# w2 in transfers of 8, 4 and 1 blocks, and the result on every eighth partition

## The chip, the core and the metric

The kernel runs on one core of a Trainium2 chip. A core has five engines that run their own instruction streams and meet at semaphores: TensorE (PE in the profile, its weight loads PEld), VectorE (DVE), ScalarE (ACT), GpSimd (POOL) and SyncE (SP, which here only issues transfers), beside 16 DMA engines that move data between the chip's memory (HBM) and the core's on-chip memory. The metric is device time in microseconds of one execution, the median of several.

## What is computed

One decode step of a transformer block for four sequences: attention over a cache of 4096 keys and values in 32 heads, then a dense layer with a mish activation. `_A` is the attention, `_B` the dense layer; the change touches only `_B` and the end of the kernel.

```python
B, Sq, D, F = 4, 1, 640, 1728;  H, Sk, Dh = 32, 4096, 128

def _A_ref(x, k_cache, v_cache, wq, wo):
    q = (x @ wq).reshape(B, Sq, H, Dh).transpose(0, 2, 1, 3)
    scores = einsum("bhqd,bhkd->bhqk", q, k_cache) * (Dh ** -0.5)
    o = einsum("bhqk,bhkd->bhqd", softmax(scores), v_cache)
    return o.transpose(0, 2, 1, 3).reshape(B, Sq, H * Dh) @ wo

def _B_ref(x, w1, b1, w2):
    h = einsum("bsd,df->bsf", x, w1) + b1
    sp = log1p(exp(-abs(h))) + where(h > 0, h, 0)
    return einsum("bsf,fd->bsd", h * tanh(sp), w2)

h  = x + _A_ref(layernorm(x), k_cache, v_cache, wq, wo)
h2 = h + _B_ref(layernorm(h), w1, b1, w2)          # the output, 4 x 640, bf16
```

## The kernel before

**Staging.** K and V are 268 MB of the 283 MB that the kernel reads. They pass through three large on-chip buffers (`slot`), 8 MB per transfer, in units of 8 heads of one sequence; 16 units in all. Per unit VectorE multiplies K with the query (L677), TensorE sums the products (L689), softmax follows (L726 to L774), and TensorE multiplies with V (L799). The steady part of this runs in hardware loops.

**The order of work** is written out by hand. The class `Program` records operations with what they read and write, works out the semaphore waits from that, and emits each engine's operations in the order in which they were added. So the order in the code is the order on each engine. All loads of weights and of K and V are issued from SP and go through one DMA queue, in the order of issue.

**The end of the kernel** reuses two of the slots. `wend` takes wo and w1, `wend2` takes w2 and, behind it, all small intermediate tiles (`scratch`). The weights are asked for by `load` (L907), which waits until the slot's readers are done and issues the transfer from SP (L916): wo in two parts, w1 in three, then the last 64 rows of w2 (L941, after a memset on GpSimd at L935 that clears the other partitions), then w2's 13 full blocks of 128 rows.

**How w2 lies.** F = 1728 rows are 13 blocks of 128 (`C2`) and 64 more. `W2P` says which blocks one transfer takes: 0 to 5, 6 to 9, 10 and 11, 12. Blocks go in pairs: a pair is 256 rows, and partition p holds rows 2p and 2p + 1 of it, so a row of the transfer is 2 x 640 bf16 values, 2,560 bytes in one piece. A block is thus every second row of 256. Block 12 and the rest are whole.

**What has to agree with it.** The activations of block c must lie on the partitions on which w2's rows of block c lie. `f_rows(c)` (L546) gives those rows as a slice; it is used where b1 is turned (L608, at the start of the kernel) and where w1 is applied: `h1_pass` (L1089) takes `w1_sb[:, dc, f_rows(c)]` as the stationary operand, 14 blocks for each of 5 chunks of D, 70 matmuls with 4 columns to stream (one for each sequence). The slices step by 2 elements (4 bytes) for blocks 0 to 11 and by 1 for the others. `d_rows` (L475) does the same for w1's own rows.

**From w1 to the output.** `hT` holds the residual sum h, transposed (L1059); its column means and variances come through TensorE (L1074). The w1 pass runs on TensorE around the variance, then the residual is put into the accumulator `y2` (L1164), then VectorE and ScalarE compute mish into `act_t` (L1123 to L1151, the last is one of the two instructions at L1134). A small matmul (L1192) and a ScalarE copy (L1196) move the last 64 activations to every second partition. Then `w2_products` (L1173): for each block four matmuls, one for each quarter of the 640 output columns, which go to partitions 32t to 32t + 3 of `y2`, for t = 0 to 3. The order is blocks 0 to 5, the rest, 6 to 9, 10 and 11, 12. Four copies, two on VectorE and two on ScalarE (`gather`, L1204), bring the quarters side by side onto four partitions, and SP stores them (L1213).

Of the kernel before, what the change touches and what calls it, by code (L numbers as in the profile page):

```python
# [8 lines left out]
BF16 = mybir.dt.bfloat16  # L9
ACT = mybir.ActivationFunctionType  # L10
ALU = mybir.AluOpType
# [223 lines left out]
def kernel(  # L235
# [13 lines left out]
    nc = tc.nc  # L249

    B, Sq, D = A_x.shape
    _, H, Sk, Dh = A_k_cache.shape
    F = B_w1.shape[1]
    N = B * Sq
    DC = D // 128
# [23 lines left out]
    C2 = F // 128  # L279
    FM = C2 * 128  # L280
    FREM = F - FM
    FC = C2 + 1
    W2P = (0, 6, 10, 12, C2)
    W1P = (0, 2, 4, DC)
    OT4 = 4
    DT = D // OT4
    OVER = 128 - FREM


# [14 lines left out]
    s_bank, tr_bank, qq_bank, o_bank, oT_bank = banks[0:4], *banks[4:8]  # L304
    S_BANK, TR, QQ, OB, OT = [("bank", i) for i in range(4)], *[("bank", i) for i in range(4, 8)]
# [5 lines left out]
    ident_f = const([128, 128], FP32, "ident_f")  # L311
# [48 lines left out]
    def load_kv(what, rows, u, i, parts=1):  # L360
        w = SLOT // parts
        for k in range(parts):
# [26 lines left out]
        w=cells(0, 0, o0),  # L389
# [5 lines left out]
        w=["b1"],  # L395
# [10 lines left out]
            out=ident[:, :],  # L406
            in_=ident[:, :],
# [6 lines left out]
        r=["ident"],  # L414
        w=["ident"],
# [4 lines left out]
        r=["ident"],  # L420
        w=["ident_f"],
# [12 lines left out]
    def bn_stats():  # L434
        for s in range(2):
# [7 lines left out]
        r=["stats"],  # L443
        w=["mv"],
# [4 lines left out]
            out=ln_std[:, :], in_=ln_mv[:, 1:2], func=ACT.Sqrt, bias=eps_t[0:N, :], scale=1.0  # L449
        ),  # L450
        r=["mv", "eps"],
        w=["std"],
# [4 lines left out]
        r=["std"],  # L457
        w=["rstd1"],
# [4 lines left out]
            out=ln1_bf,  # L463
# [6 lines left out]
        r=["x", "mv", "rstd1"],  # L470
        w=["ln1"],
# [12 lines left out]
    def turn_rows(src):  # L484
        for c in range(DC):
# [9 lines left out]
            out=q_sel[:, :, :],  # L495
            in_=ident[:, :].rearrange("p (t r) -> p t r", t=CT)[:, :, 0:N],
        ),
        r=["ident"],
        w=["q_sel"],
    )  # L500
    for src, dst, r, w in (
# [7 lines left out]
            r=[OT],  # L509
            w=[w],  # L510
# [3 lines left out]
    def identity_sums(dst, pattern, name, **kw):  # L514
# [13 lines left out]
            out=own[:, :], in0=own1[:, :], scalar1=-1.0, scalar2=1e30, op0=ALU.add, op1=ALU.mult  # L528
        ),
        r=["own1"],  # L530
        w=["own"],
# [7 lines left out]
        r=["dq_f"],  # L539
        w=["dq_m"],  # L540
# [3 lines left out]
    )  # L544

    def f_rows(c):  # L546
        if c < C2 - C2 % 2:
            f0 = c // 2 * 256 + c % 2
            return slice(f0, f0 + 255, 2)
        f0 = c * 128 if c < C2 else F - 128  # L550
        return slice(f0, f0 + 128)


    assert CT == NO
# [15 lines left out]
    for k in range(HC):  # L570
# [4 lines left out]
                out=q_rows[:, k * 512 : (k + 1) * 512], in_=s_bank[k][:, :]  # L575
            ),
            r=[S_BANK[k]],
            w=[("qrows", k)],
# [3 lines left out]
    def q_turned():  # L582
        for g in range(G):
# [14 lines left out]
            out=qT[:, 0 : NU * G].rearrange("p (o b g) -> p o b g", o=NO, b=N),  # L598
            in_=qT_ps[:, :, :, :].rearrange("p g o b -> p o b g"),
        ),  # L600
        r=[QQ],
        w=["qT"],
# [292 lines left out]
    i1, i2, i3 = slot_of(NU - 1), slot_of(NU - 2), slot_of(NU - 3)  # L895
    wend, wend2 = slot[i1], slot[i2]
# [4 lines left out]
    nw2 = FC * D  # L901
    w2_sb = wend2[:, 0 : C2 * D].rearrange("p (k n) -> p k n", k=C2)
    w2r_sb = wend2[:, C2 * D : nw2]
    C2E = C2 - C2 % 2
    w2_view = B_w2[0 : C2E * 128, :].rearrange("(m p k) n -> p m (k n)", p=128, k=2)

    def load(out_ap, in_ap, i, lo, hi, name, sem=None):  # L907


        ops = {}  # L910
        for cell in cells(i, lo, hi):
            for d in P.readers.get(cell, {}).values():
                ops[d.nth] = d
        P.add(
            "SP",
            lambda: nc.sync.dma_start(out=out_ap, in_=in_ap),  # L916
            w=[name],
            sem=sem or "_".join(map(str, name)),
            after=ops.values(),
        )  # L920
# [3 lines left out]
    for k0, k1 in zip(W1P, W1P[1:]):  # L924
# [11 lines left out]
        w=["w2r"],  # L936
# [5 lines left out]
        w=["w2r"],  # L942
        sem=f"slot{i2}",
    )
    for k0, k1 in zip(W2P, W2P[1:]):
        if k0 < C2E:
            assert k0 % 2 == k1 % 2 == 0
            to = wend2[:, k0 * D : k1 * D].rearrange("p (m n) -> p m n", n=2 * D)
            of = w2_view[:, k0 // 2 : k1 // 2]
        else:  # L950
            to, of = w2_sb[:, k0, :], B_w2[k0 * 128 : k1 * 128, :]
        load(to, of, i2, k0 * D, k1 * D, ("w2", k0))

    at = [nw2]

    def scratch(n, dt=FP32):
        a = at[0]
        w = n * (2 if dt == FP32 else 1)
        w += w % 2
        at[0] = a + w  # L960
        ap = wend2[:, a : a + w]
        return ap.bitcast(FP32)[:, 0:n] if dt == FP32 else ap[:, 0:n]

    def do(eng, emit, r=(), w=()):

        return P.add(eng, emit, r=r, w=w, after=[last_pv])
# [88 lines left out]
    def cols(n=DC, dt=FP32):  # L1055
        return scratch(n * N, dt).rearrange("p (c n) -> p c n", c=n)

    hT = cols()
    tt(hT, xT_res[:, :, :], yT[:, :, :], ALU.add, ["xT_res", S_BANK[0]], ["hT"])  # L1059

    def column_means(src, name):
        part = scratch(N)
        m_ps = oT_bank[:, 0:N]
        do(
            "DVE",
            lambda: nc.vector.tensor_reduce(
                out=part, in_=src.rearrange("p c n -> p n c"), axis=AX.X, op=ALU.add
            ),
            [name],
            [name + "_part"],  # L1070
        )
        do(
            "PE",
            lambda: nc.tensor.matmul(m_ps, lhsT=mean_f[:, :], rhs=part, start=True, stop=True),  # L1074
            [name + "_part", "mean_f"],
            [OT],
        )
        return m_ps

    m_ps = column_means(hT, "hT")  # L1080
    h2T, hc, sq = cols(dt=BF16), cols(), cols()
    for dst, w in ((h2T, "h2T"), (hc, "hc")):
# [17 lines left out]
    for dc in range(DC):  # L1100
        w1 = ("w1", max(k0 for k0 in W1P if k0 <= dc))
        do("PE", lambda dc=dc: h1_pass(dc), [w1, "h2T"], [QQ])
        if dc == 1:
# [4 lines left out]
                    out=std, in_=v_ps, func=ACT.Sqrt, bias=eps_t[:, :], scale=1.0  # L1108
# [10 lines left out]
            do("DVE", lambda: nc.vector.reciprocal(out=rstd, in_=std), ["std2"], ["rstd"])  # L1119

    h1n, h1s, ta, tb, tc_, td = (cols(FC) for _ in range(6))
    act_t = cols(FC, BF16)
    tt(  # L1123
        h1n, h1_ps, rstd.unsqueeze(1).to_broadcast([128, FC, N]), ALU.mult, [QQ, "rstd"], ["h1n"]
    )
# [5 lines left out]
    def stt(out_, a, scalar, b, op0, op1, r, w):  # L1131
        do(
            "DVE",
            lambda: nc.vector.scalar_tensor_tensor(  # L1134
                out=out_, in0=a, scalar=scalar, in1=b, op0=op0, op1=op1
            ),
            r,
            w,
        )
# [5 lines left out]
            out=tc_, in0=tb, scalar1=-0.5, scalar2=-1.0, op0=ALU.mult, op1=ALU.add  # L1145
# [2 lines left out]
        ["tc"],  # L1148
    )
    do("DVE", lambda: nc.vector.reciprocal(out=td, in_=tc_), ["tc"], ["td"])  # L1150
    stt(act_t, td, 1.0, h1s, ALU.add, ALU.mult, ["td", "h1s"], ["act"])  # L1151


    y2 = s_bank[1][:, 0:DT]

    def residual():
        for t in range(OT4):
            for c in range(DC):
                d0, step = d_rows(c).start, d_rows(c).step
                p0 = max(0, -(-(t * DT - d0) // step))  # L1160
                p1 = min(128, -(-((t + 1) * DT - d0) // step))
                if p0 < p1:
                    d = d_rows(c, p0, p1)
                    ins = nc.tensor.matmul(  # L1164
                        y2[32 * t : 32 * t + N, d.start - t * DT : d.stop - t * DT : step],
                        lhsT=hT[:, c, :],
                        rhs=ident_f[:, p0:p1],
                        start=(d.start == t * DT),
                        stop=False,
                    )  # L1170
        return ins

    def w2_products(blocks):  # L1173
        for c in blocks:
            w2, h = (w2_sb[:, c, :], act_t[:, c, :]) if c < C2 else (w2r_sb, act_r)
            for t in range(OT4):
                ins = nc.tensor.matmul(
                    y2[32 * t : 32 * t + N, :],
                    lhsT=h,
                    rhs=w2[:, t * DT : (t + 1) * DT],  # L1180
                    start=False,
                    stop=(c == C2 - 1),
                )
        return ins

    do("PE", residual, ["hT", "ident_f"], [S_BANK[1]])

    act_r = scratch(N, BF16)
    r_ps = oT_bank[:, 0:N]
    do(  # L1190
        "PE",
        lambda: nc.tensor.matmul(r_ps, lhsT=apart, rhs=act_t[:, C2, :], start=True, stop=True),  # L1192
# [3 lines left out]
    do("ACT", lambda: nc.scalar.copy(out=act_r, in_=r_ps), [OT], ["act_r"])  # L1196
    for k0, k1 in zip(W2P, W2P[1:]):
        do("PE", lambda b=range(k0, k1): w2_products(b), [("w2", k0), "act"], [S_BANK[1]])
        if k0 == 0:
            do("PE", lambda: w2_products([C2]), ["w2r", "act_r"], [S_BANK[1]])  # L1200
    out_bf = scratch(D, BF16)[0:N, :]

    def gather(t, copy):
        return lambda: copy(  # L1204
            out=out_bf[:, t * DT : (t + 1) * DT], in_=y2[32 * t : 32 * t + N, :]
        )

    for t in range(OT4):
        eng, copy = (("DVE", nc.vector.tensor_copy), ("ACT", nc.scalar.copy))[t % 2]
        do(eng, gather(t, copy), [S_BANK[1]], [("out_bf", t)])  # L1210
    P.add(
        "SP",
        lambda: nc.sync.dma_start(out=out.rearrange("b s d -> (b s) d"), in_=out_bf),  # L1213
        r=[("out_bf", t) for t in range(OT4)],
        sem="out",
    )

# [41 lines left out]
```

## Time and profile before

| | |
|---|---|
| median of 3 runs | 664.91 us (664.72 to 665.21) |
| the profiled execution | 664.55 us |
| its span, first to last instruction | 662.8 us |
| read from HBM in the span | 283.35 MB, 428 GB/s |
| PE / DVE / ACT / POOL busy, share of the span | 58% / 53% / 14% / 0% |
| TensorE's granted clock, mean | 0.804 |

The profile is of one execution. Its rows give start and duration in microseconds from the start of the span, engine, source line, operation, and the tiles written and read with their shapes (partitions x elements). "idle before" tells how long the engine stood before the instruction and what ended that. A granted clock of 0.50 means that TensorE had half of its full speed. The chain of waits is followed back from the last instruction: at each step to what released it. The columns of the windows are: the stretch and its length, busy time and number of instructions of PE, PEld, DVE, ACT and POOL, granted clock, share of the DMA engines, GB/s.

The weights of the end, as they are issued and land (from the list of DMA issues and SP's timeline):

| transfer | KB | issued at, us | us to landing |
|---|---|---|---|
| w2, last 64 rows | 80 | 625.42 | 28.7 |
| w2, blocks 0 to 5 | 960 | 626.01 | 30.5 |
| w2, blocks 6 to 9 | 640 | 626.64 | 31.5 |
| w2, blocks 10 and 11 | 320 | 637.54 | 21.5 |
| w2, block 12 | 160 | 646.3 | 13.1 |

### The profile page before, as it was taken

Reading aid. Unit: us, or ns where it says so; the run is one execution under the profiler, and the core shown is the slowest. Engines: PE = TensorE matmul, PEld = TensorE weight load, DVE = VectorE, ACT = ScalarE, POOL = GpSimd, SP = SyncE. Lnnn points to the kernel's source line nnn. Section 1 sums busy time; section 2 is a strip of 40 time slices with the busy share of each in tenths; the row PEclk is TensorE's granted clock in tenths of the full one; section 3 lists DMA queues with packets and bytes.
Section 4 is the critical chain, followed back from the end, with each engine's and each line's share of the span. In section 5 each row is a group of like instructions: output and inputs, shape, how many; then the busy total and the mean of one; then the engine's idle time right before and its main releaser. Section 6 shows DMA issues by size and latency. Waiting matters only on the chain.

```text
span 662.8 us, 6698 instructions
## 1 busy us (share of the span) xinstructions
PE 381.4 (58%) x2692; PEld 171.6 (26%) x2692; DVE 352.6 (53%) x315; ACT 90.3 (14%) x321; POOL 2.8 (0%) x14
## 2 busy tenths in 40 slices
PE   0364868375481837548183754818375481837675
PEld 0121323132230313223031322303132230313344
DVE  2085868184573818457381845738184572818502
ACT  0202020202002020200202020020202002020211
POOL 1000000000000000000000000000000000000000
PEclk9778889879695987969598796958879695887955
DMA  9999999999999999999999999999999999999997
GB/s 380 443 440 439 443 405 427 444 431 440 435 427 419 443 439 431 435 439 427 423 443 427 443 435 431 423 435 439 431 435 439 427 423 443 431 439 435 409 421 288
DMA packets 6685, 283.52 MB, mean 428 GB/s; under 512 B 713, under 2 KB 913, under 8 KB 2066
## 3 DMA queue, kind: packets, MB, share of 16 engines
q1 hardware_dynamic: 6664, 283.35, 99.2%
q8 instruction: 8, 0.13, 0.1%
q14 instruction: 3, 0.02, 0.0%
q10 hardware_dynamic: 10, 0.01, 0.0%
HBM read 283.35 MB, written 0.01 MB: 428 GB/s over the span
## 4 chain that ended last, share of the span: by engine, by line
DMA 44%; DVE 25%; PE 19%; another core or an unknown queue 6%; issue 2%; SPq 2%; ACT 1%; DVEq 0%; POOL 0%; ACTq 0%
DMA slot<-in_A_k_cache_dram 41%; DVE slot L677 21%; PE bank L689 13%; PE bank L799 5%; DMA slot<-in_B_w_dram 3%; DVE s_sb L664 3%; SPq L916 2%; ACT e L774 1%; PE bank L757 0%; DVE mx L744 0%; DVE rl L851 0%; PE bank L735 0%; DVE otn L858 0%; DVEq L228 0%
## 5 line engine op out<-in xcount | busy, mean ns | idle before, releaser
L689 PE MATMUL bank<-slot,ident 128*128 128x512 bf16 x1024 | 273.6, 422 | 242.3 <-DVE slot L677 242.3
L677 DVE TENSOR_TENSOR slot<-slot,qb 128x4096 bf16<-128x4096 bf16 x128 | 288.3, 2284 | 152.5 <-DMA slot<-in_A_k_cache_dram 148.1
L689 PEld LDWEIGHTS bank<-slot,ident 128*128 128x128 bf16 x1024 | 101.2, 107 | 399.9 <-DVE slot L677 274.7
L664 DVE TENSOR_REDUCE s_sb<-bank 128x64 f32<-128x512 f32 x64 | 44.0, 688 | 58.3 <-PE bank L689 58.3
L774 ACT ACTIVATE e<-s_sb,nb 128x256 bf16<-128x256 f32 x128 | 63.1, 494 | 44.2 <-DVE nb L766 44.2
L799 PE MATMUL bank<-slot,e 128*32 128x512 bf16 x1024 | 61.8, 395 | 4.4 <-DMA slot<-in_A_v_cache_dram 2.7
L644 ACT CAST qb<-bank 128x128 bf16<-128x128 f32 x17 | 4.5, 266 | 307.5 <-PE bank L635 307.5
L799 PEld LDWEIGHTS bank<-slot,e 128*32 128x32 bf16 x1024 | 26.6, 99 | 37.7 <-issue 9.6
L819 ACT COPY o_sb<-bank 128x512 f32<-128x512 f32 x16 | 9.4, 586 | 183.4 <-PE bank L799 183.4
L744 DVE TENSOR_REDUCE mx<-bank 1x8 f32<-1x128 f32 x16 | 4.5, 278 | 39.9 <-PE bank L735 39.9
L774 ACT ACTIVATION_READ_ACCUMULATOR e<-s_sb,nb 128x1 f32 x128 | 23.8, 186 | 0.0
L832 PE MATMUL bank<-sel,o_sb 128*128 128x8 f32 x136 | 18.5, 262 | 0.0
L832 PEld LDWEIGHTS bank<-sel,o_sb 128*128 128x128 f32 x136 | 17.4, 200 | 0.0
L851 DVE RECIPROCAL rl<-bank 128x8 f32<-128x8 f32 x17 | 3.4, 202 | 15.4 <-PE bank L832 15.4
L561 PE MATMUL bank<-slot,xT 128*32 128x512 bf16 x40 | 4.5, 631 | 10.7 <-DMA slot<-in_A_wq_dram 10.7
L757 PE MATMUL bank<-mx,nscale 1*128 1x8 f32 x32 | 6.1, 262 | 5.9 <-DVE mx L744 5.9
L618 DVE COPY b1T<-bank 128x14 f32<-128x14 f32 x1 | 0.2, 173 | 15.1 <-PE bank L608 15.1
L830 PEld LDWEIGHTS bank<-rs,ones_f 128*128 128x128 f32 x34 | 6.5, 197 | 3.8 <-ACT o_sb L819 1.6
L757 PEld LDWEIGHTS bank<-mx,nscale 1*128 1x128 f32 x32 | 4.7, 182 | 10.6 <-DVE mx L744 10.6
L726 DVE TENSOR_REDUCE pm<-s_sb 128x1 f32<-128x256 f32 x16 | 6.7, 420 | 0.5
L735 PE MATMUL bank<-ident_f,pm 128*1 128x128 f32 x32 | 6.1, 272 | 1.2 <-DVE pm L726 1.2
L766 DVE TENSOR_TENSOR nb<-bank,own 128x8 f32<-128x8 f32 x16 | 2.7, 167 | 7.6 <-PE bank L757 7.6
(85 smaller groups left out, 68.8 us busy)
## 6 DMA issues: line engine op xcount, KB each, us to landing
slot<-in_A_v_cache_dram SPq DMA_DIRECT2D x2, 4096.0 KB, 44.6
slot<-in_A_wq_dram SPq DMA_DIRECT2D x1, 5120.0 KB, 15.3
slot<-in_A_wo_dram SPq DMA_DIRECT2D x2, 2560.0 KB, 32.8
slot<-in_B_w_dram SPq DMA_DIRECT2D x2, 864.0 KB, 33.1
slot<-in_B_w_dram SPq DMA_DIRECT2D x1, 960.0 KB, 30.5
slot<-in_B_w_dram SPq DMA_DIRECT2D x1, 640.0 KB, 31.5
slot<-in_B_w_dram SPq DMA_DIRECT2D x1, 432.0 KB, 32.3
slot<-in_B_w_dram SPq DMA_DIRECT2D x1, 320.0 KB, 21.5
```

The lines of the kernel that those rows point to most:

```text
L664: lambda: nc.vector.tensor_reduce(out=s_sb[:, part * RP : (part + 1) * RP], in_=s_bank[part][:, :].rearrange("p (r w) -> p r w", w=W), axi ...
L677: return nc.vector.tensor_tensor(out=kt, in0=kt, in1=qbs[u % NS][:, k * DQ : (k + 1) * DQ] .unsqueeze(1) .to_broadcast([128, RP, DQ]), op= ...
L689: ins = nc.tensor.matmul(s_bank[part][:, :].rearrange("p (r w) -> p r w", w=W), lhsT=ident[:, :], rhs=kt[:, :, d : d + W], start=(d == 0), ...
L726: lambda: nc.vector.tensor_reduce(out=pm[:, :], in_=s_sb[:, :], axis=AX.X, op=ALU.max),
L735: lambda: nc.tensor.matmul(tr_bank[0:1, 0:128], lhsT=pm[:, :], rhs=ident_f[:, :], start=True, stop=True),
L757: lambda: nc.tensor.matmul(nb_ps, lhsT=nscale[:, :], rhs=mx[:, :], start=True, stop=True),
L774: ins = nc.scalar.activation(out=e2[:, :, h, :], in_=s_sb[:, :].rearrange("p (g r) -> p g r", r=RQ), func=ACT.Exp, bias=nb[:, h : h + 1], ...
L799: ins = nc.tensor.matmul(o_bank[t : t + G * RQ, :], lhsT=e2[:, g, :, :], rhs=vt[:, g * RQ : (g + 1) * RQ, :], start=(g < CT), stop=(g >= N ...
L819: lambda: nc.scalar.copy(out=o_sb[:, :], in_=o_bank[:, :]),
L830: nc.tensor.matmul(l_ps, lhsT=ones_f[:, :], rhs=rss[u % NS][:, :], start=True, stop=True)
L832: ins = nc.tensor.matmul(o_ps, lhsT=o_sb[:, r * Dh : (r + 1) * Dh], rhs=sel[:, r, :], start=(r == 0), stop=(r == RQ - 1),)
L916: lambda: nc.sync.dma_start(out=out_ap, in_=in_ap),
```

## The change

w2's full blocks go in three transfers, of 8, 4 and 1 blocks. In a transfer of n blocks, partition p holds n consecutive rows of w2, so its piece is n x 1,280 bytes. `f_rows` follows from the same table: it steps by 8, 4 and 1 elements.

The stationary operands of the residual and of the w2 products become 32 columns wide, zero but for every eighth column, which holds one of the four sequences. They come from two new tiles that GpSimd clears: `hW`, into which GpSimd copies `hT`, and `act_t`, which is now 32 wide itself and is written by VectorE with a step. So the products fill all 128 partitions of `y2`, and sequence b's quarter t lies on partition 32t + 8b. One copy on ScalarE takes all of `y2` out, and the store picks every eighth partition.

```diff
-    W2P = (0, 6, 10, 12, C2)
+    W2P = (0, 8, 12, C2)
...
+    OS = 32 // N
...
     def f_rows(c):
-        if c < C2 - C2 % 2:
-            f0 = c // 2 * 256 + c % 2
-            return slice(f0, f0 + 255, 2)
-        f0 = c * 128 if c < C2 else F - 128
-        return slice(f0, f0 + 128)
+        for k0, k1 in zip(W2P, W2P[1:]):
+            if k0 <= c < k1:
+                return slice(k0 * 128 + c - k0, k1 * 128 - (k1 - 1 - c), k1 - k0)
+        return slice(F - 128, F)
...
     for k0, k1 in zip(W2P, W2P[1:]):
-        if k0 < C2E:
-            assert k0 % 2 == k1 % 2 == 0
-            to = wend2[:, k0 * D : k1 * D].rearrange("p (m n) -> p m n", n=2 * D)
-            of = w2_view[:, k0 // 2 : k1 // 2]
-        else:
-            to, of = w2_sb[:, k0, :], B_w2[k0 * 128 : k1 * 128, :]
-        load(to, of, i2, k0 * D, k1 * D, ("w2", k0))
+        load(
+            wend2[:, k0 * D : k1 * D],
+            B_w2[k0 * 128 : k1 * 128, :].rearrange("(p k) n -> p (k n)", p=128),
+            i2, k0 * D, k1 * D, ("w2", k0),
+        )
...
+    hW = scratch(DC * 32).rearrange("p (c n) -> p c n", c=DC)
+    act_t = scratch(FC * 32, BF16).rearrange("p (c n) -> p c n", c=FC)
+    for t, name in ((hW, "hW"), (act_t, "act")):
+        do("POOL", lambda t=t: nc.gpsimd.memset(t, 0.0), w=[name])
     hT = cols()
     tt(hT, xT_res[:, :, :], yT[:, :, :], ALU.add, ["xT_res", S_BANK[0]], ["hT"])
...
+    do("POOL", lambda: nc.gpsimd.tensor_copy(out=hW[:, :, ::OS], in_=hT), ["hT", "hW"], ["hW"])
...
-    act_t = cols(FC, BF16)
...
-    stt(act_t, td, 1.0, h1s, ALU.add, ALU.mult, ["td", "h1s"], ["act"])
+    stt(act_t[:, :, ::OS], td, 1.0, h1s, ALU.add, ALU.mult, ["td", "h1s", "act"], ["act"])
...
-                        y2[32 * t : 32 * t + N, d.start - t * DT : d.stop - t * DT : step],
-                        lhsT=hT[:, c, :],
+                        y2[32 * t : 32 * t + 32, d.start - t * DT : d.stop - t * DT : step],
+                        lhsT=hW[:, c, :],
...
-                    y2[32 * t : 32 * t + N, :],
+                    y2[32 * t : 32 * t + 32, :],
...
-    act_r = scratch(N, BF16)
-    r_ps = oT_bank[:, 0:N]
+    act_r = scratch(32, BF16)
+    r_ps = oT_bank[:, 0:32]
...
-    out_bf = scratch(D, BF16)[0:N, :]
-
-    def gather(t, copy):
-        return lambda: copy(
-            out=out_bf[:, t * DT : (t + 1) * DT], in_=y2[32 * t : 32 * t + N, :]
-        )
-
-    for t in range(OT4):
-        eng, copy = (("DVE", nc.vector.tensor_copy), ("ACT", nc.scalar.copy))[t % 2]
-        do(eng, gather(t, copy), [S_BANK[1]], [("out_bf", t)])
+    out_bf = scratch(DT, BF16)
+
+    do("ACT", lambda: nc.scalar.copy(out=out_bf, in_=y2), [S_BANK[1]], ["out_bf"])
     P.add(
         "SP",
-        lambda: nc.sync.dma_start(out=out.rearrange("b s d -> (b s) d"), in_=out_bf),
-        r=[("out_bf", t) for t in range(OT4)],
+        lambda: nc.sync.dma_start(
+            out=out.rearrange("b s (t n) -> t (b s) n", t=OT4),
+            in_=out_bf[::OS, :],
+        ),
+        r=["out_bf"],
         sem="out",
     )
```

More of the change, by code (lines that the diff above doesn't have):

```diff
@@ L903 @@
     w2r_sb = wend2[:, C2 * D : nw2]
-    C2E = C2 - C2 % 2
-    w2_view = B_w2[0 : C2E * 128, :].rearrange("(m p k) n -> p m (k n)", p=128, k=2)
     def load(out_ap, in_ap, i, lo, hi, name, sem=None):
@@ L945 @@
     for k0, k1 in zip(W2P, W2P[1:]):
-        if k0 < C2E:
-            assert k0 % 2 == k1 % 2 == 0
-            to = wend2[:, k0 * D : k1 * D].rearrange("p (m n) -> p m n", n=2 * D)
-            of = w2_view[:, k0 // 2 : k1 // 2]
-        else:
-            to, of = w2_sb[:, k0, :], B_w2[k0 * 128 : k1 * 128, :]
-        load(to, of, i2, k0 * D, k1 * D, ("w2", k0))
+        load(
+            wend2[:, k0 * D : k1 * D],
+            B_w2[k0 * 128 : k1 * 128, :].rearrange("(p k) n -> p (k n)", p=128),
+            i2,
+            k0 * D,
+            k1 * D,
+            ("w2", k0),
+        )
     at = [nw2]
@@ L1184, in w2_products @@
         return ins
-    do("PE", residual, ["hT", "ident_f"], [S_BANK[1]])
-    act_r = scratch(N, BF16)
-    r_ps = oT_bank[:, 0:N]
+    do("PE", residual, ["hW", "ident_f"], [S_BANK[1]])
+    act_r = scratch(32, BF16)
+    r_ps = oT_bank[:, 0:32]
     do(
```

## The prediction

> **What bounds the kernel now.** I read the DMA row of the page first, then the chain of waits, then the timeline of the last ten microseconds.
>
> ```profile
> DMA  9999999999999999999999999999999999999997
> ```
>
> The 16 DMA engines are busy from the first slice to the last: 283.35 MB at 428 GB/s. Nothing in the change touches the loop over K and V or its bytes, so whatever it does happens in the last slice. The chain of waits ends there:
>
> ```profile
> 637.54 21.46 DMA slot<-in_B_w_dram
> 659.04 0.74 PE bank L1177 x12
> 659.81 0.31 DVE slot L1204
> 660.13 0.32 DVE slot L1204
> ```
>
> The columns are start, duration and what. The end is set by the last landings of w2, the last three rounds of w2 products, then two copies one behind the other on VectorE. After them comes the store. The timeline, on its way there:
>
> ```profile
> 652.29 0.89 PE L1091 MATMUL bank<-slot,slot 128*128 128x4 bf16 x28 [0.36 <-DVE slot L969]
> 653.46 1.26 PE L1091 MATMUL bank<-slot,slot 128*128 128x4 bf16 x42
> 654.65 1.01 PE L1164 MATMUL bank<-ident_f,slot 128*4 128x80 f32 x22
> 656.61 0.22 DVE L1134 SCALAR_TENSOR_TENSOR slot<-slot 128x56 bf16<-128x56 f32 x1
> 656.93 0.16 PE L1192 MATMUL bank<-slot 128*128 128x4 bf16 x1 [1.27 <-issue]
> 657.02 2.73 PE L1177 MATMUL bank<-slot 128*4 128x160 bf16 x56
> 658.23 0.36 PEld L1177 LDWEIGHTS bank<-slot 128*4 128x4 bf16 x16 [0.44 <-DMA slot<-in_B_w_dram]
> 659.04 0.10 PEld L1177 LDWEIGHTS bank<-slot 128*4 128x4 bf16 x8 [0.45 <-DMA slot<-in_B_w_dram]
> 659.45 0.09 PEld L1177 LDWEIGHTS bank<-slot 128*4 128x4 bf16 x4 [0.31 <-DMA slot<-in_B_w_dram]
> 660.48 0.34 SPq L1213 DMA_DIRECT2D out_dram<-slot  x1
> ```
>
> Two paths meet in the w2 products. One is the arithmetic: the w1 pass (L1091), the activation, ready at 656.61 + 0.22 = 656.83, and from 657.02 the products. The other is the landing of w2: TensorE waits for blocks 6 to 9 until 658.23, for 10 and 11 until 659.04, for block 12 until 659.45. The first six blocks are there at 656.5 (issued at 626.01, 30.5 to land), 0.3 us before the activation. So the arithmetic trails the data by little, and a delay of it is soon on the path.
>
> **The change, part by part.**
>
> *w2 in larger pieces.* 12 blocks now come in rows of 2,560 B. They will come in rows of 10,240 B (8 blocks) and 5,120 B (4). What row length is worth is read from the windows over stretches in which one kind of row was moving (wo in 20 KB, w1 in 6.9 KB, then w2); the last two columns are the share of the DMA engines and GB/s:
>
> ```profile
> 644.00:648.50 4.50, 2.30 (x84) 2.22 (x84) 0.30 (x1) 0.00 (x0) 0.00 (x0) 0.50 0.99 416
> 648.50:651.50 3.00, 2.45 (x81) 2.37 (x81) 0.36 (x2) 0.00 (x0) 0.00 (x0) 0.50 0.98 399
> 653.00:657.00 4.00, 2.73 (x74) 2.39 (x71) 1.75 (x7) 1.89 (x4) 0.00 (x0) 0.50 1.04 395
> ```
>
> GB/s over share gives 420 for 20 KB, 407 for 6.9 KB, 380 for w2. Eight blocks are 1.31 MB: 3.45 us at 380, 3.17 at 413 (10 KB, between the two rows). Four blocks: 0.66 MB, 1.72 against 1.66 at 395. That is 0.34 us less; bounds 0.2 (all at 395) and 0.5 (all at 420). The landings become: blocks 0 to 7 midway between 656.5 and 658.23, less 0.28, at 657.09; 8 to 11 at 659.04 - 0.34 = 658.70; block 12 at 659.11. SP issues one transfer fewer; it stands 10.46 us in an issue at 626.64, but the engines stay full meanwhile, so I count nothing.
>
> *The products.* 56 matmuls as before, in rounds of four that run side by side. Seven rounds go from 657.02 to about 658.12, one takes 0.33 (659.45 to 659.78): 0.13 us a round and 0.19 for the first to come through. Their weights grow from 4 to 32 columns. L799 already has 32-column weights: 32 matmuls of 512 in 3.61 us at clock 0.50, (3.61 - 0.19) / 8 = 0.43 a round, which is 0.13 for 160 columns. So 0; at most 56 x 14 ns = 0.8 us, by the mean load of 118 ns at L799 against 104 at L1177.
>
> *The result.* Two copies in turn on each of two engines, 659.81 to 660.46, become one ScalarE copy of 128x160. Between 266 ns (128x128, L644) and 586 (128x512, L819) that is 293 ns. PE's end to the store's issue shrinks from 0.70 to 0.34: 0.36 saved.
>
> *The store.* 16 pieces of 320 B in place of 4 of 1,280 B; its 5 KB stay. Issue 0.34 us, then 1.95 to the end of the span. I take it as equal, with bounds of -0.1 and +0.2 from the spread of issue times (0.33 at L366 to 0.56 at L385). The Trainium skill ("DMA: Bandwidth & Descriptors", Specifications) says that below 512 B the engine reads, modifies and writes; no run here shows its price, and the sum leaves it out.
>
> *GpSimd.* Two memsets after 625.9 (0.2 to 0.5 us each by L973 and L426; GpSimd then has nothing until 651) and one copy of hT at 651.07, some 0.26 us (L976). The residual that needs it starts at 654.65, so 3 us cover it. At worst the copy holds up VectorE's sum at 651.10 by 0.26. The SP queue's load of w2's last rows waits for the memset at L935, which stays ahead of the new ones.
>
> *The residual.* 22 matmuls in 1.01 us, weights 32 columns wide instead of 4. Loads of 128 four-byte columns take 227 ns at the same clock (L832: eight in 1.83); a quarter is 57, against some 30 now: +0.6 us at most. PE is idle from 655.66 to 656.90, which hides it, and that gap moves along with the w1 pass.
>
> *The columns of w1.* This is the part that the short description does not name. w1's columns must meet w2's rows, so f_rows now steps by 8 elements (16 B) for blocks 0 to 7, by 4 (8 B) for 8 to 11, and by 1 after; it was 2 and 1. The w1 pass loads these columns as weights, 5 x 14 = 70 loads of 128 columns with 4-column matmuls, so the load is the whole time: (1.26 - 0.17) / 41 = 27 ns each, with steps 2 and 1 alike. PE runs it without a gap from 652.29 to 654.65 ahead of the activation. One place in the trace has a wider step, L486 at the start: five loads with a step of 5 elements (10 B), then five with 2 and 1.
>
> ```profile
> 4.38 0.35 PE L486 MATMUL bank<-ident,slot 4*128 4x4 bf16 x5 [4.38 <-DVE slot L462]
> 5.09 0.27 PE L486 MATMUL bank<-ident,slot 4*128 4x4 bf16 x5 [0.36 <-DVE xT L508]
> ```
>
> With 178 and 162 ns for a single one, that is (0.35 - 0.18) / 4 = 43 ns a load against 27. A step of 10 B costs 16 ns more. Carried on in a line (2.7 ns per byte beyond 4), 16 B gives 59 and 8 B 38; in proportion to the step, 69 and 34. Then 40 loads x 32 to 42 + 20 x 7 to 11 = 1.5 to 1.8 us; I take 1.6. Bounds: 0 (the price has nothing to do with the step), and 114 ns a load, half of the 227 ns of a four-byte load, for all 60: 60 x 87 = 5.2 us. The Trainium skill speaks against the change here: "SBUF — State Buffer", Door 1, has lines of 16 B and wants at least two hits on each. A step of 16 B leaves one hit; if a load then takes twice 27 ns and a step of 8 B stays free, the delay is 1.1 us and the whole change comes to 0. L486 agrees in direction.
>
> The same step is in b1's turn (L608, 14 loads in 0.41 us at 21.5): +0.5 us, and the first multiplication waits for K until 35.42, so 0.
>
> **The sum.** Data path: blocks 8 to 11 at 658.70, five rounds 0.65 + 0.19 + 0.02, so products end at 659.56; copy and hand-over 0.34, store at 659.90, 0.58 earlier than 660.48. Arithmetic path with a w1 delay d: first product at 657.02 + d, 14 rounds 1.82 + 0.19, end 659.03 + d, store at 659.37 + d. It decides from d = 0.53. With d = 1.6 the store is issued at 660.97, 0.49 us later than now. Against the profiled execution's 664.55 that is 665.04; that execution lies 0.36 below the median of 664.91, so I forecast 665.4. What w2 and the copy gain (about 1.1 us on the arithmetic path) is given back by w1's loads.
>
> **The rivals.**
> 1. *The step is free or cheap*: at most L486's 16 ns for any wide step, d of 0 to 0.96. For it: steps 1 and 2 cost the same 27 ns. Against it: L486 itself. -0.58 to -0.15, 664.3 to 664.8.
> 2. *The wide step makes the load one column at a time* (slower). 114 ns a load for 40 of them, d = 40 x 87 = 3.5: +2.4 us, 667.3; for 60, +4.1, 669.0. It decides by more than 0.2% from d = 2.44, 88 ns a load. For it: the step grows far beyond any row of this trace. Against it: at 10 B the load is still well below 114.
> 3. *The store is longer by its small pieces*: at its own issue-to-end of 2.29 us, if pieces double the 1.95 that follows the issue, +1.95 on the sum, 667.4; half of that, 666.4. For it: nothing in the trace; against: 5 KB in all.
> 4. *w2's rows are cut up again and land as now*: the data path then ends only 0.36 earlier than today, and the sum, set by the arithmetic, stays at 665.4; the page's count of packets under 8 KB would stay at 2,066.
>
> **How the numbers follow.** 0.2% of the time is 1.33 us, about what a measurement of this kernel can tell from no change. Forecast (50 to 88 ns a load at the wide step, -0.1 to +1.3): 0.45, within 0.2%. Rival 1: 0.15, of it 0.04 faster by more. Rival 2: 0.32, slower. Rival 3: 0.06, of it 0.04 slower. Rival 4: 0.02, no change. Faster 0.04, same 0.60, slower 0.36. The range runs from rival 1's low end, 664.2, to 667.6, just past the first value of rival 2; the likeliest case's own range is 664.8 to 666.2.
>
> **What would show it.** L1091 (then by its new line) is the test: 70 loads over 2.1 us now, some 3.7 with the forecast, 5.6 with rival 2. The products should then run in one piece with no wait for w2 inside; waits for DMA there speak for rival 1. The copy should take 0.29, the store stay at 2.3 us to the end. Wrong altogether if the loop's first 620 us differ.

## The result and the profile after

The changed kernel takes 666.06 us (median of 22 runs, 665.6 to 668.05) against 664.90 us of the kernel before (22 runs): a ratio of 1.0017, with a 95% interval of 1.0010 to 1.0023. That is 1.16 us slower, within the 0.2% named in the prediction, and clear of its own interval.

The profiled execution is a long one, 667.25 us with a span of 665.4, so the two spans should not be subtracted. Of their 2.6 us, 1.57 lie before the landing of the second half of wo (TensorE takes it up at 650.13, before at 648.56). They arise in the loop over K and V: wo's first half is asked for at 612.73, before at 610.72. The change touches only one operation ahead of that, the turn of b1 at the start: it takes 0.82 us instead of 0.50, and the first multiplication, which waits for K, still starts at 35.36 (before at 35.42). The forecast's sign of being wrong altogether, a difference in the first 620 us, does not hold either: with the same b1 and the same loop, e2_w2_only asks for wo at 610.45 and e10_rows at 610.90 (both below). So the late start is this execution's own, and the runs leave open where it comes from; 1.2 us is also what this execution has over its median. From wo's landing on the two can be compared. Two rows of the kernel before that are needed for it (start, duration, engine, line, operation):

```profile
648.56 2.29 PE L1025 MATMUL bank<-slot,slot 128*128 128x4 bf16 x80 [2.26 <-DMA slot<-in_A_wo_dram]
...
654.76 0.22 DVE L969 TENSOR_TENSOR slot<-bank,slot 128x56 f32<-128x56 f32 x1 [0.64 <-PE bank L1091]
```

The timeline of the changed kernel:

```profile
650.13 2.29 PE L1024 MATMUL bank<-slot,slot 128*128 128x4 bf16 x80 [3.53 <-DMA slot<-in_A_wo_dram]
...
653.87 1.49 PE L1096 MATMUL bank<-slot,slot 128*128 128x4 bf16 x28 [0.36 <-DVE slot L968]
...
655.64 2.15 PE L1096 MATMUL bank<-slot,slot 128*128 128x4 bf16 x42
...
657.72 1.21 PE L1168 MATMUL bank<-ident_f,slot 128*32 128x80 f32 x22
657.82 0.22 DVE L968 TENSOR_TENSOR slot<-bank,slot 128x56 f32<-128x56 f32 x1 [1.53 <-PE bank L1096]
...
659.62 0.41 DVE L1138 SCALAR_TENSOR_TENSOR slot<-slot 128x56 bf16<-128x56 f32 x1
...
660.09 0.21 PE L1196 MATMUL bank<-slot 128*128 128x32 bf16 x1 [1.17 <-DVE slot L1138]
...
660.23 2.06 PE L1181 MATMUL bank<-slot 128*32 128x160 bf16 x56
...
662.34 0.29 ACT L1207 CAST slot<-bank 128x160 bf16<-128x160 f32 x1 [1.82 <-PE bank L1181]
662.66 0.68 SPq L1210 DMA_DIRECT2D out_dram<-slot  x1
```

The two parts of the w1 pass are 0.60 and 0.89 us longer than the 0.89 and 1.26 before. The write of the activation takes 0.41 where it took 0.22. The 56 products run in one piece, with no wait for w2. The store's issue takes 0.68 where it took 0.34. Stage by stage, from the rows here and those shown of before:

| stage | before | after | difference |
|---|---|---|---|
| second half of wo to the w1 pass | 3.73 | 3.74 | +0.01 |
| w1 pass, until VectorE has its sums | 2.47 | 3.95 | +1.48 |
| mish, until the small matmul | 2.17 | 2.27 | +0.10 |
| small matmul to the last product | 2.85 | 2.20 | -0.65 |
| copy, until the store is issued | 0.70 | 0.37 | -0.33 |
| store, issue to end of span | 2.29 | 2.72 | +0.43 |
| sum | 14.21 | 15.25 | +1.04 |

The sum agrees with the +1.16 of the medians, whose interval is 0.7 to 1.5 us. The chain of waits shows the same: in place of the landing of w2 it now holds the landing of wo, and behind that the arithmetic, with no gap of more than 0.05 us.

```profile
617.73 32.35 DMA slot<-in_A_wo_dram
...
655.78 2.02 PE bank L1096 x42
...
660.09 0.21 PE bank L1196
660.30 2.02 PE bank L1181 x46
662.32 0.02 issue
662.34 0.29 ACT slot L1207
```

The transfers did what the change says. The page counts 1,422 packets under 8 KB where it had 2,066. The window from 653 to 657 has 415 GB/s at a share of 1.00, but w1's last part moves in it until 655.4 (issued at 623.53, 31.9 us to landing). The window behind that has w2's blocks 0 to 7 alone:

```profile
653.00:657.00 4.00, 3.64 (x61) 3.58 (x62) 0.81 (x5) 1.17 (x2) 0.00 (x0) 0.50 1.00 415
655.40:657.00 1.60, 1.60 (x31) 1.60 (x32) 0.18 (x1) 1.17 (x2) 0.00 (x0) 0.50 1.01 417
```

417 over 1.01 is 413 GB/s, where w2 in short rows had 395 at 1.04, that is 380. w2's last block lands 31.2 us after its issue at 629.53, that is 10.60 us after TensorE takes up wo; before it was 10.86 (646.32 + 13.1, and 648.56). So the data comes about 0.26 us sooner.

### The profile page after: what moved, and what is told of

Same layout as the page of the kernel before. It is cut to its first block, busy times and chain, and to the rows that moved or that the text cites. A ratio compares the mean times of both kernels' runs of the same rounds, so it can differ in the third digit from the quotient of the medians.

```text
span 665.4 us, 6698 instructions
## 1 busy us (share of the span) xinstructions
PE 381.1 (57%) x2692; PEld 172.6 (26%) x2692; DVE 352.1 (53%) x313; ACT 90.2 (14%) x320; POOL 3.6 (1%) x17
## 2 busy tenths in 40 slices
DMA packets 6169, 283.52 MB, mean 426 GB/s; under 512 B 713, under 2 KB 909, under 8 KB 1422
## 4 chain that ended last, share of the span: by engine, by line
DMA 46%; DVE 24%; PE 20%; another core or an unknown queue 7%; issue 2%; ACT 1%; DVEq 0%; SPq 0%; ACTq 0%
DMA slot<-in_A_k_cache_dram 41%; DVE slot L677 21%; PE bank L689 13%; DMA slot<-in_A_wo_dram 5%; PE bank L799 5%; DVE s_sb L664 3%; ACT e L774 1%; PE bank L1096 1%; PE bank L1024 0%; PE bank L1181 0%; PE bank L757 0%; DVE mx L744 0%; PE bank L735 0%; DVE rl L851 0%
## 6 DMA issues: line engine op xcount, KB each, us to landing
slot<-in_B_w_dram SPq DMA_DIRECT2D x1, 432.0 KB, 31.9
```

## The experiments

e1_pairs, e2_w2_only, e7_threes and e8_fours ran 11 times each; their medians are given, and ratios to the kernel before on the same chip, with 95% intervals. The others ran once, and what counts in them is single rows of the profile.

**One side at a time.** The first kernel keeps the result side of the change and puts w2 and f_rows back to pairs:

```diff
-    W2P = (0, 8, 12, C2)
+    W2P = (0, 6, 10, 12, C2)
...
+        if c < C2 - C2 % 2:
+            f0 = c // 2 * 256 + c % 2
+            return slice(f0, f0 + 255, 2)
```

> The changed kernel with w2 in pairs of rows as before (pieces of 2,560 B, f_rows with steps 2 and 1); the wide operands, the one copy and the new store stay. Theory (the wide step of w1's columns costs the time): the 70 loads of the w1 pass go back to 27 ns each, 1.5 us less than in the changed kernel, and the products again wait for w2's last block; result about 665.0 us (664.7 to 665.4), level with the kernel before. Rival (the result side costs it: the step in the activation's write, the store in 16 pieces): it stays near the changed kernel, 665.8 to 666.2, with the w1 pass at 27 ns a load.

The second keeps the w2 side alone; it is the kernel before with the new W2P, f_rows and transfers.

> The kernel before with w2 in transfers of 8, 4 and 1 blocks and the f_rows that goes with them; the narrow operands, four copies and old store stay. Theory: loads of 60 ns at 16 B and 31 ns at 8 B, the activation 1.5 us later, products in one piece to 1.5 us after where they could end now (659.0), so 0.75 us more than before: 665.6 us (665.3 to 666.0). Rival (result side): 664.5 to 664.9, as the w2 pieces land 0.3 us earlier.

Measured: e1_pairs 665.02 us, ratio 1.0001 (0.9992 to 1.0010); e2_w2_only 665.50 us, ratio 1.0011 (1.0002 to 1.0020). Both fall where the theory of the wide step had them, and the rival is out by both. From wo's landing to the end of the span it is 14.21 us before, 14.32 in e1_pairs, 15.00 in e2_w2_only and 15.25 in the changed kernel: the sides alone add up to 0.90 of the 1.04 us. The timeline of e1_pairs:

```profile
653.49 1.26 PE L1098 MATMUL bank<-slot,slot 128*128 128x4 bf16 x42
...
656.63 0.41 DVE L1140 SCALAR_TENSOR_TENSOR slot<-slot 128x56 bf16<-128x56 f32 x1
...
657.24 2.56 PE L1183 MATMUL bank<-slot 128*32 128x160 bf16 x56
...
660.16 0.68 SPq L1212 DMA_DIRECT2D out_dram<-slot  x1
```

and of e2_w2_only:

```profile
654.13 2.18 PE L1089 MATMUL bank<-slot,slot 128*128 128x4 bf16 x42
...
658.15 0.22 DVE L1132 SCALAR_TENSOR_TENSOR slot<-slot 128x56 bf16<-128x56 f32 x1
...
658.56 2.04 PE L1175 MATMUL bank<-slot 128*4 128x160 bf16 x56
...
661.33 0.34 SPq L1211 DMA_DIRECT2D out_dram<-slot  x1
```

With steps of 2 and 1 the w1 pass is back at 1.26 in the wide kernel. With the wide step it is at 2.18 in the narrow one. The result side brings two costs of its own in e1_pairs, the write of 0.41 and the issue of 0.68. There the write is covered: the products still end at 657.24 + 2.56 = 659.80, since they wait for w2. In the changed kernel nothing covers it, which is most of what the two sides alone leave out. The products in one piece take 2.04 us with 4-column weights and 2.06 with 32: the width costs nothing.

**What a step costs.** Two kernels with other widths of the transfers, `W2P = (0, 12, C2)` and `W2P = (0, 3, 8, 12, C2)`:

> The changed kernel with w2 in transfers of 12 and 1 blocks: f_rows steps by 12 elements (24 B) for 12 blocks. One look at the loads of the w1 pass (60 at 24 B, 10 at 2 B). Theory (each load pays for every column that lies apart from the one before it, and 16 B is already the full price): 60 ns a load as at 16 B, w1 pass about 60 x 60 + 10 x 27 ns = 3.9 us. Rival (price in proportion to the step, from 43 at 10 B and 60 at 16 B): some 85 to 95 ns a load, w1 pass 5.4 to 6.0 us.

> The changed kernel with w2 in transfers of 3, 5, 4 and 1 blocks: f_rows steps by 6, 10, 8 and 2 B. One look at the loads of the w1 pass. Theory (full price only where each column lies in its own 16 B): 27 ns at 6 B, about 40 at 10 B as in the turn of the input at the start, 31 at 8 B. Rival (in proportion to the step): 27 ns up to 6 B, 38 at 10 B, 30 at 8 B; the two differ at e3, not here, and this run only says whether the row of the start that the forecast used holds for the w1 pass.

Measured in one execution each: e3_step12 666.37 us, e4_steps35 664.99. The second part of the w1 pass (3 chunks of D, 42 loads) in e3_step12 and in e4_steps35:

```profile
654.43 2.43 PE L1096 MATMUL bank<-slot,slot 128*128 128x4 bf16 x42
```

```profile
654.02 1.54 PE L1096 MATMUL bank<-slot,slot 128*128 128x4 bf16 x42
```

A row starts with its first matmul, when that one's load is done, so it holds 41 of the 42 loads. From each, 0.17 us goes off for the last matmul, and 27 ns for every load with a step of up to 6 B. In e3_step12, 35 loads at 24 B share 2.26 - 0.16 = 2.10 us: 60 ns each. In e4_steps35, 15 loads at 10 B are left with 1.37 - 0.38 - 0.40 = 0.59 us (8 at 6 B and 6 at 2 B take 27, 12 at 8 B take 33, from e8_fours below): 39 ns. In the changed kernel 23 loads at 16 B are left with 1.98 - 0.40 - 0.16 = 1.42: 62 ns. The price does not grow beyond 16 B, so it is not in proportion to the step. That was the rival in e3_step12, with 5.4 to 6.0 us for the whole pass; its two parts took 1.69 + 2.43 = 4.12, near the theory's 3.9.

**Rows of three and four.** If a small step is cheap, w2 can still have longer pieces. Both are the kernel before with, for n of 3 or 4, `W2P = (0, 6, 9, 12, C2)` or `(0, 8, 12, C2)`, n rows in one piece of the transfer, and

```diff
-            f0 = c // 2 * 256 + c % 2
-            return slice(f0, f0 + 255, 2)
+            f0 = c // n * n * 128 + c % n
+            return slice(f0, f0 + 127 * n + 1, n)
```

> The kernel before with w2's rows in threes (pieces of 3,840 B; transfers of 6, 3, 3 and 1 blocks) and f_rows with a step of 3 elements (6 B); all else as before. Theory (a step of up to 6 B is free, 27 ns a load; larger pieces land sooner): w1 pass as before, w2's last block lands some 0.2 us sooner, 664.6 us (664.4 to 664.8), 0.1 to 0.3 under the kernel before. Rival (what w2 gains is hidden or the loads pay): level with before or above.

> The kernel before with w2's rows in fours (pieces of 5,120 B; transfers of 8, 4 and 1 blocks) and f_rows with a step of 4 elements (8 B); all else as before. Theory: 60 loads at 33 ns make the w1 pass 0.35 us longer, which the wait for w2 covers (the products could start at 657.4 and would still be held by the block that lands last); 664.7 us (664.5 to 665.0), level with before. Rival (every delay of the w1 pass is on the path): 665.2 or more.

Measured: e7_threes 664.90 us, ratio 1.0000 (0.9991 to 1.0009); e8_fours 664.94, ratio 1.0005 (0.9996 to 1.0014). In the profile of e7_threes:

```profile
648.72 2.29 PE L1025 MATMUL bank<-slot,slot 128*128 128x4 bf16 x80 [2.27 <-DMA slot<-in_A_wo_dram]
...
653.63 1.26 PE L1091 MATMUL bank<-slot,slot 128*128 128x4 bf16 x42
...
659.47 0.09 PEld L1177 LDWEIGHTS bank<-slot 128*4 128x4 bf16 x4 [0.20 <-DMA slot<-in_B_w_dram]
```

and of e8_fours:

```profile
653.78 1.50 PE L1091 MATMUL bank<-slot,slot 128*128 128x4 bf16 x42
...
659.15 0.84 PE L1177 MATMUL bank<-slot 128*4 128x160 bf16 x20 [0.21 <-DMA slot<-in_B_w_dram]
...
660.71 0.34 SPq L1213 DMA_DIRECT2D out_dram<-slot  x1
```

A step of 6 B is free (1.26 as before). The last block of w2 comes 10.75 us after wo (659.47 - 648.72), before 10.89 (659.45 - 648.56): 0.14 sooner, in the profile alone; the interval of the ratio is wider than that. The theory had 664.4 to 664.8 us for e7_threes; 664.90 is outside, and its rival, level with before, holds. So nothing here beats the kernel before. At 8 B a load takes (1.50 - 0.17 - 0.16) / 35 = 33 ns. The whole pass is 0.39 us longer in e8_fours (1.04 and 1.50 against 0.89 and 1.26), and the store is issued 11.99 us after wo instead of 11.92 (wo is taken up at 648.72 here too): the wait for w2 hides most of that delay, as expected.

**The store.** Its issue grew from 0.34 to 0.68, which the forecast had not allowed for. Three kernels, each with another store and one quarter of the output in it:

```diff
-            out=out.rearrange("b s (t n) -> t (b s) n", t=OT4), in_=out_bf[::OS, :],
+            out=out.rearrange("b s d -> (b s) d")[:, 0:DT], in_=out_bf[0:32:OS, :],    # e6
+            out=out.rearrange("b s d -> (b s) d")[:, 0:DT], in_=out_bf[0:N, :],        # e9
+            out=out.rearrange("b s d -> (b s) d"), in_=out_w[0:32:OS, :],              # e10
```

`out_w` is a tile of 640 columns that GpSimd clears and whose first 160 are `out_bf`.

> The changed kernel, storing only the first quarter of the columns: 4 pieces of 320 B from partitions 0, 8, 16 and 24; the other three quarters of the output are left out. One look at the store alone. Theory (the issue grows with the store's two-part pattern on the output, 16 pieces): the issue takes 0.34 us as before the change, and the span ends 2.3 us after the issue begins. Rival (it is the small piece of 320 B, or the step of 8 partitions): the issue stays at 0.68 and 2.7 us to the end.

> The changed kernel, storing 4 pieces of 320 B from the neighbouring partitions 0 to 3 to the first quarter of the four output rows (values are not the output's, three quarters are left out). One look at the store's issue: before the change 0.34 us (4 whole rows of 1,280 B, partitions 0 to 3), in the changed kernel 0.68, with 4 pieces from partitions 0, 8, 16, 24 0.73. Theory now (the step between the partitions makes the issue long): 0.34. Rival (the piece of 320 B, or the gaps between pieces in HBM): about 0.7.

> The changed kernel, storing 4 whole rows of 1,280 B from partitions 0, 8, 16 and 24 of a wider tile that is cleared and holds the first quarter only (the other three quarters of the output are left out). Theory (step between partitions): issue about 0.7. Rival (piece or gaps in HBM): 0.34.

One execution each took 666.26, 665.38 and 665.88 us. SP's row of the store in e6_store4, e9_next and e10_rows:

```profile
661.75 0.73 SPq L1210 DMA_DIRECT2D out_dram<-slot  x1
```

```profile
661.45 0.34 SPq L1210 DMA_DIRECT2D out_dram<-slot  x1
```

```profile
661.26 0.72 SPq L1212 DMA_DIRECT2D out_dram<-slot  x1
```

The first theory, that the 16 pieces make the issue long, fell with e6_store4: 4 pieces took 0.73. The second held. With neighbouring partitions the issue takes 0.34 for pieces of 320 B with gaps in HBM (e9_next), and with every eighth partition 0.72 for whole rows (e10_rows). To the end of the span it is 2.15 us in e9_next (span 663.6) and 2.75 in e10_rows (664.0). So the step between partitions costs the time, not the size or number of the pieces. Only the step of eight was run; what a smaller one costs stays open.

## Why the prediction was right, and where not

The forecast was 665.4 us, no change within 0.2%, with rather a loss than a gain; it came to 666.06.

- **The columns of w1** were the right mechanism and nearly the right size: a delay of 1.6 us was forecast, 1.48 came. The 62 ns at 16 B and 33 at 8 B lie within or just under the forecast's 59 to 69 and 34 to 38. That the line through 10 B came near, with 59, was luck, since e3_step12 shows that there is no line: 27 ns up to 6 B, 33 at 8, 39 at 10, 62 at 16, 60 at 24. The rule of the Trainium skill ("SBUF — State Buffer", Door 1: lines of 16 B, two hits wanted on each) has the right shape, with a full price from one hit per line on. Its size, which the forecast took as double, is 2.3 times 27 ns, and two hits, at 8 B, are not quite free.
- **w2 in larger pieces**: 413 GB/s as in the forecast, and the data 0.26 us sooner against 0.34. On the changed kernel's path it is worth nothing by itself, as the arithmetic ends later than the data. What shows is the products without their waits, -0.65, and that comes from their later start: they begin 10.10 us after wo (660.23 - 650.13) and need the last block near the end of their 2.06 us, where the old pieces had it at 10.89. By these rows the old pieces would have been in time too; that kernel, a late start with the old pieces, was not run.
- **The copy** came as forecast: -0.33 against -0.36.
- **The store is the step that was mis-sized.** It was taken as equal, +0.2 at most; it is +0.43, of which 0.34 is the issue and 0.09 stays open. The bound was read from issues whose partitions are neighbours. The rows held at most a weak hint: the load of w2's last 64 rows (L941) goes to every second partition and took 0.55 to issue, where the loads of K and V took 0.33, but the load of w2's blocks 0 to 5, to neighbouring partitions, took 0.58. The three other stores show the cause of the longer issue. With this, "one copy" gains nothing: -0.33 at the copy, +0.43 at the store.
- **The write of the activation** was not in the sum: 0.41 against 0.22 us, as every value goes 16 B after the one before it. It is on the path in the changed kernel. 0.10 of the 0.19 remains in the stage; the rest is won back at hand-overs, at ScalarE's exponential (0.04 us after VectorE instead of 0.10; before, ScalarE's dummy activation ran until 655.42 and may have held it up, which no run shows) and at the small matmul (0.06 instead of 0.10).
- **GpSimd, the wide weights, the residual** at nothing: right. GpSimd's copy ran 0.22 us beside VectorE's sum, which kept its 0.19. The residual took 1.21 instead of 1.01 and still ended before the activation.
- Rival 1 (a free step) fell with e1_pairs and e2_w2_only, rival 2 (one column at a time, 114 ns) with the row of L1096. Rival 3 had the right place, the store, and the wrong reason and size: it priced small pieces at +1.95, and 4 of them from neighbouring partitions cost nothing in e9_next. Rival 4 fell with the packet count.

The two store and write terms, 0.43 and 0.10, are what the forecast of +0.49 lacks to the +1.04 of the profile. The other terms cancel, by luck: the delay of the w1 pass was put 0.12 too large, and the products with their hand-over (2.20 instead of 2.10) and the copy (0.37 instead of 0.34) 0.13 too small.

## What to carry to other kernels

A layout that suits a transfer is paid for by whoever reads in step with it: look at the address step it puts into stationary operands, into VectorE's writes and between the partitions of a store, and price each from a row with that step. Longer pieces are worth it only as far as the landing is still what the end waits for; here 0.26 us of data time stood against 1.5 us of weight loads. Rows of three blocks, a step of 6 B, would have had the longer pieces without the loads' price, and still changed nothing that can be measured.

## What the runs showed of the hardware

- A load of 128 stationary columns in bf16 at a granted clock of 0.50 takes 27 ns with a step of 2 to 6 B between columns, 33 at 8 B, 39 at 10 B, 60 to 62 at 16 and 24 B. The row of the start that the forecast used (L486) ran at a granted clock of 1.00 and gives 43 ns at 10 B and 27 below, nearly the same.
- A store's issue on SP takes 0.34 us from neighbouring partitions (4 pieces of 320 or 1,280 B) and 0.68 to 0.73 from every eighth (16 pieces of 320 B, or 4 of 320 or 1,280 B).
- VectorE's write of 128x56 values in bf16 takes 0.22 us packed and 0.41 with a step of 16 B.
